# Second-layer weight pieces loaded from GpSimd's queue, and twelve copies of transposed probabilities moved to VectorE

## The chip, the cores and the metric

The kernel runs on one core of a Trainium2 chip. The metric is the device time of one execution in microseconds (us). Before the change, three runs gave a median of 1055.12 us (1054.56 to 1058.52).

## What is computed

Three functions one behind the other, in float32 with float64 weights from the host:

```python
# attention: batch 4, heads 8, sequence 576, head_dim 64
scores = scale * np.matmul(q, k.transpose(0, 1, 3, 2))
scores = np.where(block_i >= block_j, scores, -1000000000.0)   # blocks of 64
attn = np.exp(scores - np.max(scores, axis=-1, keepdims=True))
x = np.matmul(attn / (np.sum(attn, axis=-1, keepdims=True) + 1e-09), v)
x = x.transpose(0, 2, 1, 3).reshape(B * S, H * D)              # 2304 x 512
# first layer, d_ff = 1536
x = ((x @ w_a) * (x @ w_b)) @ w_out
# second layer, d_ff = 1536
xn = x / np.sqrt(np.mean(x * x, axis=-1, keepdims=True) + 1e-06) * rms_g
g = xn @ w_gate
out = (g / (1.0 + np.exp(-g)) * (xn @ w_val)) @ w_out
```

## The kernel before

**Engines and names.** PE multiplies matrices. ACT (ScalarE), DVE (VectorE) and POOL (GpSimd) work on tiles of 128 partitions. SP (SyncE) issues transfers. A float32 operand is split into a high and a low part in a faster format, and a product is three matmuls. Each engine carries out its instructions in the order in which a scheduler placed them when the program was built, and a waiting instruction holds up all behind it on its engine.

**Attention.** Sixteen pairs of heads (four per batch) go through the same steps: PE scores a group of 64 queries of both heads (L455, from batch 2 on L463), DVE takes the row maximum (L478), ACT the exponential into `pp` with its row sum (L484), DVE the reciprocal of the sums (L492, L493), POOL scales `pp` (L496, nine tiles per pair of heads), PE transposes it (L521), and the transposed tile is copied out of PSUM (L523). In batch 0 (`whole`) that copy into `pw` is one ACT copy, and the product with the values follows (L546). In the other batches ACT copies the high part and DVE subtracts to get the low part (L527, values at L590). Batch 0 stands alone in the first 57 us or so. Batches 1 to 3 are interleaved with the matmuls of the first layer (L705 to L707) until about 445 us. The values of a batch are loaded into `vr` (L401) and split on POOL (L114, L427) into `vv`.

**Weights.** Each weight arrives as float64 in a tile of 512 KB, here called a piece. `decode` makes float32 of it: ACT scales the low word in place (L146), ACT turns the high word into `a` (L149), DVE shifts (L150), POOL adds (L151), after which the buffer of the piece is free. The 36 pieces of the second layer use two buffers `st` in turn: 24 of w_gate and w_val ("ab"), each one transfer (L188), and 12 of w_out ("o"), each four transfers of 128 KB (L186). So piece i + 2 can be loaded only when POOL has added piece i. They are decoded in the background of the first layer (4 in its second block, 8 in its third, 24 in its last). Two pieces at a time are combined for a Strassen-Winograd product (`combine`: DVE L233 and L234, POOL L235 and L236, ACT L239 and L240 for the high part, POOL L242 for half of the low part) and stored to DRAM by SP (L244). From about 660 us the second layer streams them back in.

The pieces of the first layer (tiles `ld` and `st`) go through the same function.

Of the kernel before, what the change touches and what calls it, by code (L numbers as in the profile page):

```python
# [12 lines left out]
AF = mybir.ActivationFunctionType  # L13
# [3 lines left out]
P = 128  # L17
# [34 lines left out]
def tile_attention_moe_moe(  # L52
# [13 lines left out]
    pe, act, dve, pool, sp = nc.tensor, nc.scalar, nc.vector, nc.gpsimd, nc.sync  # L66
# [4 lines left out]
    NTH, TF = w_o1.shape[:2]  # L71
# [4 lines left out]
    w_ab, w_o = (w_ab1, w_ab2), (w_o1, w_o2)  # L76
# [48 lines left out]
    gate = {}  # L125
# [46 lines left out]
    def stage_loads(n):  # L172
        while len(staged) + prepared[0] < min(n, len(w_pieces)):
            i = len(staged) + prepared[0]
            layer, kind, f, y = w_pieces[i]
            if layer == 0 and i % LANDING < LANDING - 2:
                if not landing:
                    landing.append(stage.tile([P, LANDING - 2, 4 * P], I64, tag="bg", name="ld", bufs=1))
                st = landing[0][:, i % LANDING]
            else:  # L180
                st = stage.tile([P, 4 * P], I64, tag="st", name="st", bufs=2)
            if kind == "o" and layer == 1:

                for dm in range(KC):
                    z, o = divmod(dm * TF + f % TF, KC)
                    sp.dma_start(out=st[:, dm * P:dm * P + P], in_=w_o[1][f // TF, z, :, o * P:o * P + P])  # L186
            else:
                sp.dma_start(out=st, in_=(w_ab if kind == "ab" else w_o)[layer][f, y])  # L188
            staged[i] = st

    def prepare():

        i = prepared[0]
        if i >= len(w_pieces):
            return
        stage_loads(min(i + min(2 + i, LANDING), max(len(w_pieces) // 2, i + 2)))
        layer, kind, f, y = w_pieces[i]
        w = 4 * P
# [98 lines left out]
    def blocks_of(part, j):  # L297

        return [b for b in PARTS[part] if b >= 2 * j]
# [8 lines left out]
    def attention(pools, x_of, done):  # L308
# [6 lines left out]
        st = [small[:, x, 0:NQ + 2] for x in range(2)]  # L315
# [18 lines left out]
        def single(m):  # L334
            return m >= FIRST_SINGLE
# [163 lines left out]
        def p_transposes(u):  # L499
            m, part = divmod(u, 2)  # L500
            places = PLACE[part]
            whole = m // (H // 2) < WHOLE
            if whole:
                pt[u] = [ap.tile([P, len(places) * P], F32, tag=f"ph{part}", name=f"pw{part}")]
            else:
                pt[u] = [ap.tile([P, len(places) * P], F32R, tag=f"p{x}{part}", name=f"p{x}{part}") for x in "hl"]
            if single(m) and part == 1:

                groups = [[(j, b) for j in js for b in blocks_of(1, j)] for js in ((0,), (1,), (2,), (3, 4))]
            else:  # L510
                groups = [places[at:at + 4] for at in range(0, len(places), 4)]
            at = 0
            for group in groups:
                ps = ps_t()
                n = len(group) * P
                for x, (j, b) in enumerate(group):
                    to = ps[:, x * P:(x + 1) * P]
                    if single(m) and part == 1 and x < 3:
                        by_head = ps[:, 0:3 * P].rearrange("p (h n) -> p h n", h=2)
                        to = by_head[:, :, P:P + Q] if b == NQ - 1 else by_head[:, b % 2, 0:P]  # L520
                    pe.transpose(to, pp[b][:, j * P:(j + 1) * P], ident)  # L521
                hi = pt[u][0][:, at:at + n]
                gate["act"] = act.activation(hi, ps[:, 0:n], AF.Copy)  # L523
                lo = None if whole else pt[u][1][:, at:at + n]
                at += n
                if not whole:
                    dve.tensor_tensor(lo, ps[:, 0:n], hi.bitcast(F32), ALU.subtract)  # L527
                yield n / 1.2
# [76 lines left out]
        ps = ps_s()  # L605
# [7 lines left out]
        for u in range(2 * NP + 2):  # L613
            m, part = divmod(u, 2)
            if u >= 2:
                yield from (whole_values if (u - 2) // H < WHOLE else values)(u - 2)
            sc = list(SCORED[part]) if m < NP else []
            ct = p_transposes(u - 1) if 1 <= u <= 2 * NP else iter(())
            if sc:
                yield score(m, sc.pop(0))  # L620
                if len(sc) > 2:
                    yield score(m, sc.pop(0))
                if part == 0:
                    make_vv(m)
                    make_q(m, 1)
                else:
                    make_k(m + 1)
                    if m + 1 > FIRST_SINGLE:
                        make_q(m + 1, 0)
            alive = True  # L630
            while sc or alive:
                c = next(ct, None) if alive else None
                if c is None:
                    alive = False
                else:
                    yield c
                if sc:
                    yield score(m, sc.pop(0))
            if m < NP and part == 1:
                if m + 1 == FIRST_SINGLE:  # L640
                    make_q(m + 1, 0)
                load(m + 2)
# [348 lines left out]
    n = 0  # L991
# [223 lines left out]
```

## Time and profile before

| | us |
|---|---|
| median of three runs | 1055.12 |
| profiled execution | 1059.24 |
| its span, first to last instruction | 1057.4 |

The profiled execution has 1.84 us around its span and is 4.12 us above the median. PE is busy for 1040.1 us of the span (98%), DVE 697.3 (66%), ACT 618.5 (58%), POOL 426.6 (40%). Busy shares are means over stages with different limits. The rows below are therefore taken stage by stage, and a gap of PE is read by what ended it.

### The profile page before, as it was taken

What the parts mean: (1) busy time and instruction counts of PE and PEld (TensorE: products, weight loads), DVE (VectorE), ACT (ScalarE), POOL (GpSimd) and SP (SyncE); (2) the same over time, 40 slices, a digit from 0 to 9 for tenths busy, and PEclk for the clock granted to TensorE, in tenths of its full rate; (3) what the DMA queues carried; (4) which work ended last, traced back from release to release, by engine and by line L of the source; (5) the groups of instructions that cost most, each with busy time, mean ns of one, the idle gap of its engine ahead of it and who ended that gap; (6) DMA issues with size and microseconds to landing.
All of it is one profiled execution on the core that took longest, in us unless ns stands there. A gap on an engine that the chain in (4) does not pass through costs nothing.

```text
span 1057.4 us, 17005 instructions
## 1 busy us (share of the span) xinstructions
PE 1040.1 (98%) x5676; PEld 934.6 (88%) x5676; DVE 697.3 (66%) x1371; ACT 618.5 (58%) x1376; POOL 426.6 (40%) x448
## 2 busy tenths in 40 slices
PE   9989999999999999999999999999999999999998
PEld 6768887899988888888888888999999999999998
DVE  6547677777775677556587634793876838666285
ACT  7978968577576765456555322753646536355362
POOL 5856667465564564275565501120221202212020
PEclk9999999999999999999999999999999999999999
DMA  9767877978999765798889664787889887887883
GB/s 246 228 185 255 281 257 267 327 258 278 325 342 301 260 234 220 260 344 321 318 314 354 258 224 169 208 287 253 250 289 310 272 269 251 282 277 238 268 249 112
DMA packets 116379, 281.24 MB, mean 266 GB/s; under 512 B 27971, under 2 KB 40771, under 8 KB 105798
## 3 DMA queue, kind: packets, MB, share of 16 engines
q1 hardware_dynamic: 116294, 280.18, 79.6%
q8 instruction: 45, 0.74, 0.3%
q14 instruction: 40, 0.33, 0.1%
HBM read 218.77 MB, written 61.36 MB: 265 GB/s over the span
## 4 chain that ended last, share of the span: by engine, by line
PE 85%; DMA 6%; ACT 4%; DVE 2%; POOL 1%; issue 1%; SPq 0%; ACTq 0%; POOLq 0%
PE mm L733 25%; PE mm L764 12%; PE mm L706 8%; PE mm L707 8%; PE mm L705 8%; PE mm L665 4%; PE mm L667 4%; PE mm L666 4%; PE t L590 3%; PE t L521 3%; PE s L463 2%; DMA qr<-in_q_dram 2%; PE s L455 2%; PE t L546 1%; DMA st<-in_w_o_dram 1%
## 5 line engine op out<-in xcount | busy, mean ns | idle before, releaser
L705 PE MATMUL mm<-xh,ab 128*128 128x512 f32 (+1 forms) x480 | 181.4, 381 | 0.0
L707 PE MATMUL mm<-xh,ab 128*128 128x512 f32 (+1 forms) x480 | 179.7, 374 | 0.0
L706 PE MATMUL mm<-xl,ab 128*128 128x512 f32 (+1 forms) x480 | 179.5, 374 | 0.0
L733 PE MATMUL mm<-hT,w 128*128 128x384 f32 x576 | 165.6, 337 | 1.2 <-ACT mm L741 1.2
L121 POOL TENSOR_TENSOR hl<-g,hh 128x384 fp32r<-128x384 f32 x36 | 42.7, 1187 | 299.7 <-ACT hh L111 299.7
L733 PE MATMUL mm<-hB,w 128*128 128x384 f32 x432 | 125.9, 336 | 0.0
L764 PE MATMUL mm<-hh,w 128*128 128x384 f32 x504 | 125.3, 336 | 0.0
L496 POOL TENSOR_SCALAR pp<-pp,st 128x256 f32<-128x256 f32 (+4 forms) x144 | 84.2, 599 | 73.5 <-DVE st L493 44.1
L741 ACT ACTIVATE mm<-mm 128x384 f32<-128x384 f32 x144 | 66.8, 474 | 75.5 <-PE mm L733 42.5
L733 PEld LDWEIGHTS mm<-hT,w 128*128 128x128 f32 x576 | 105.9, 188 | 2.6 <-ACT mm L741 2.4
L705 PEld LDWEIGHTS mm<-xh,ab 128*128 128x128 f32 x480 | 90.4, 189 | 15.5 <-issue 0.4
L706 PEld LDWEIGHTS mm<-xl,ab 128*128 128x128 f32 x480 | 90.5, 189 | 15.0 <-issue 0.7
L707 PEld LDWEIGHTS mm<-xh,ab 128*128 128x128 f32 x480 | 90.5, 188 | 14.9 <-issue 0.2
L733 PE MATMUL mm<-lT,w 128*128 128x384 f32 x288 | 96.9, 337 | 0.0
L764 PEld LDWEIGHTS mm<-hh,w 128*128 128x128 f32 x504 | 90.7, 188 | 0.3 <-ACT mm L741 0.3
L484 ACT ACTIVATE pp<-s,st 128x288 f32<-128x288 f32 (+8 forms) x142 | 72.3, 512 | 26.3 <-DVE st L478 13.5
L764 PE MATMUL mm<-hl,w 128*128 128x384 f32 x252 | 81.5, 336 | 0.0
L733 PEld LDWEIGHTS mm<-hB,w 128*128 128x128 f32 x432 | 79.5, 188 | 0.0
L665 PE MATMUL mm<-hh,o 128*128 128x512 f32 (+1 forms) x208 | 78.3, 378 | 0.5 <-ACT hh L111 0.5
L666 PE MATMUL mm<-hh,o 128*128 128x512 f32 (+1 forms) x208 | 77.2, 372 | 0.0
L667 PE MATMUL mm<-hl,o 128*128 128x512 f32 (+1 forms) x208 | 75.7, 371 | 0.1
L733 PE MATMUL mm<-lB,w 128*128 128x384 f32 x216 | 72.6, 336 | 0.0
(161 smaller groups left out, 2431.8 us busy)
## 6 DMA issues: line engine op xcount, KB each, us to landing
w<-wc SPq DMA_DIRECT2D x252, 256.0 KB, 3.6
ab<-wab SPq DMA_DIRECT2D x36, 1024.0 KB, 8.7
w<-wco SPq DMA_DIRECT2D x126, 256.0 KB, 3.2
wc<-bg SPq DMA_DIRECT2D x12, 1792.0 KB, 7.3
o<-wo SPq DMA_DIRECT2D x12, 1536.0 KB, 9.5
st<-in_w_ab_dram SPq DMA_DIRECT2D x34, 512.0 KB, 6.8
wab<-ab SPq DMA_DIRECT2D x12, 1024.0 KB, 7.0
wco<-bg SPq DMA_DIRECT2D x6, 1792.0 KB, 6.7
```

The lines of the kernel that those rows point to most:

```text
L121: eng_lo.tensor_tensor(lo, src, hi.bitcast(F32), ALU.subtract)
L484: act.activation(pi[:, a:z], pss[x][:, 0:z - a], AF.Exp, bias=s[:, b:b + 1], scale=1.0, accum_out=t3[:, b, x:x + 1],)
L496: pool.tensor_scalar(t, t, s[:, y:y + 1], 1.0, ALU.mult, ALU.mult)
L665: pe.matmul(ps[:, 0:n], wh, hh, start=(y == 0), stop=False)
L666: pe.matmul(ps[:, 0:n], wl, hh, start=False, stop=False)
L667: pe.matmul(ps[:, 0:n], wh, hl, start=False, stop=(y == TF - 1))
L705: pe.matmul(ps[:, 0:n], wh[:, a:z], xhc, start=(c == 0), stop=False)
L706: pe.matmul(ps[:, 0:n], wh[:, a:z], xlc, start=False, stop=False)
L707: pe.matmul(ps[:, 0:n], wl[:, a:z], xhc, start=False, stop=(c == KC - 1))
L733: pe.matmul(ps, lhs, rhs[:, c, :], start=(start and c == 0 and y == 0), stop=(c == 1 and y == 2), skip_group_check=not start,)
L741: act.activation(to, ps, AF.Copy)
L764: pe.matmul(banks[m], lhs, rhs, start=(start and f == group[0] and y == 0), stop=(f == group[-1] and y == 2), skip_group_check=not start,)
```

## The change

Two edits. In `stage_loads`, the transfers of the second layer's pieces (24 of L188 and 48 of L186) are issued by POOL's queue instead of SP's. Pieces of the first layer stay on SP. In `p_transposes`, for batch 0, a copy whose place in `pw` is not a multiple of eight tiles goes to DVE, without the note for ACT's ordering (`gate`): three of the seven copies of a pair of heads, twelve in all, eight of 128x512 and four of 128x128.

```diff
@@ -183,9 +183,9 @@
                 for dm in range(KC):
                     z, o = divmod(dm * TF + f % TF, KC)
-                    sp.dma_start(out=st[:, dm * P:dm * P + P], in_=w_o[1][f // TF, z, :, o * P:o * P + P])
+                    pool.dma_start(out=st[:, dm * P:dm * P + P], in_=w_o[1][f // TF, z, :, o * P:o * P + P])
             else:
-                sp.dma_start(out=st, in_=(w_ab if kind == "ab" else w_o)[layer][f, y])
+                (pool if layer == 1 else sp).dma_start(out=st, in_=(w_ab if kind == "ab" else w_o)[layer][f, y])
             staged[i] = st
@@ -520,7 +520,10 @@
                 hi = pt[u][0][:, at:at + n]
-                gate["act"] = act.activation(hi, ps[:, 0:n], AF.Copy)
+                if whole and at % (8 * P):
+                    dve.tensor_copy(hi, ps[:, 0:n])
+                else:
+                    gate["act"] = act.activation(hi, ps[:, 0:n], AF.Copy)
```

Lines behind the second edit are three higher after the change (L526 is L523 of before, L598 is L595, L713 is L710). The scheduler places the instructions of all engines anew. At the places that the prediction speaks of, that gives the following.

POOL, around the add of the first second-layer piece (piece 0), between two pairs of heads; `pp_150` to `pp_158` are the nine scaled tiles. Before:

```order
L496 TENSOR_SCALAR pp_156<-pp_156,st 128x512
L496 TENSOR_SCALAR pp_157<-pp_157,st 128x512
L496 TENSOR_SCALAR pp_150<-pp_150,st 128x128
L496 TENSOR_SCALAR pp_151<-pp_151,st 128x128
L496 TENSOR_SCALAR pp_152<-pp_152,st 128x256
L496 TENSOR_SCALAR pp_153<-pp_153,st 128x256
L151 TENSOR_TENSOR src<-src,st 128x512
```

After:

```order
L496 TENSOR_SCALAR pp_156<-pp_156,st 128x512
L496 TENSOR_SCALAR pp_157<-pp_157,st 128x512
L151 TENSOR_TENSOR src<-src,st 128x512
L188 DMA st<-in_w_ab_dram 128x512
L496 TENSOR_SCALAR pp_150<-pp_150,st 128x128
L496 TENSOR_SCALAR pp_151<-pp_151,st 128x128
```

The add and the issue of piece 2's load that it allows now stand ahead of the four small scales instead of behind them.

ACT, the first decode step of the same piece. Before:

```order
L710 ACTIVATE asb<-mm 128x256
L523 ACTIVATE ph_2600<-t 128x384 x3
L484 ACTIVATE pp_152,st<-s,st 128x256
L484 ACTIVATE pp_153,st<-s,st 128x256
L111 ACTIVATE hh<-mm 128x256
L146 ACTIVATE st<-st 128x512
```

After:

```order
L713 ACTIVATE asb<-mm 128x256
L526 ACTIVATE ph_2600<-t 128x384
L146 ACTIVATE st<-st 128x512
L484 ACTIVATE pp_152,st<-s,st 128x256
L526 ACTIVATE ph_2600<-t 128x384
L111 ACTIVATE hh<-mm 128x256
L484 ACTIVATE pp_153,st<-s,st 128x256
```

L146 has moved ahead of two copies, two exponentials and one split. Counted over the whole order in pairs of heads (ten L484 on ACT, nine L496 on POOL), the L149 of piece 2 stood 0.16 of a pair behind the add that frees its buffer and now stands 0.60 behind it; for piece 3 it is 0.60 and 0.62, for piece 4 0.72 and 0.62, for piece 5 0.46 and 0.76.

POOL in the last block of the first layer, at two pieces whose add is followed by loads of two "o" pieces. Before:

```order
L151 TENSOR_TENSOR src<-src,st 128x512 x2
L235 TENSOR_TENSOR src<-src 128x256
L236 TENSOR_TENSOR src<-src 128x256
L242 TENSOR_TENSOR bg<-src,bg 128x3x256
L151 TENSOR_TENSOR src<-src,st 128x2x256
```

After:

```order
L151 TENSOR_TENSOR src<-src,st 128x512
L186 DMA st<-in_w_o_dram 128x128 x4
L151 TENSOR_TENSOR src<-src,st 128x512
L235 TENSOR_TENSOR src<-src 128x256
L186 DMA st<-in_w_o_dram 128x128 x4
L236 TENSOR_TENSOR src<-src 128x256
L242 TENSOR_TENSOR bg<-src,bg 128x3x256
```

Eight issues now stand among the adds and differences of `combine`. In the same stretch, each pair of "ab" loads puts two issues of L188 there. From 445 us on 46 issues (14 of L188, 32 of L186) are POOL's, between 185 and 445 us 26 (10 and 16).

## Rows read from the trace of the kernel before

**Rows 1.** Busy time by stage: start:end, length, busy us of each engine, PEclk, DMA share, GB/s.

```profile
core 0: us, PE busy (x) PEld busy (x) DVE busy (x) ACT busy (x) POOL busy (x), PEclk, DMA share, GB/s
0.00:60.00 60.00, 57.43 (x270) 42.18 (x271) 34.07 (x105) 50.30 (x143) 38.84 (x64) 1.00 0.83 241
...
185.00:235.00 50.00, 49.82 (x308) 44.20 (x307) 36.77 (x88) 32.30 (x88) 24.63 (x37) 1.00 0.87 286
235.00:300.00 65.00, 60.02 (x488) 58.72 (x488) 45.12 (x122) 42.83 (x115) 37.84 (x49) 1.00 0.96 319
300.00:445.00 145.00, 144.53 (x829) 125.77 (x828) 99.23 (x238) 90.50 (x218) 71.54 (x89) 1.00 0.79 266
445.00:600.00 155.00, 155.00 (x682) 127.12 (x681) 105.82 (x151) 81.29 (x132) 92.01 (x69) 1.00 0.87 323
...
660.00:1057.00 397.00, 393.68 (x2253) 391.96 (x2251) 263.74 (x455) 205.95 (x430) 71.82 (x58) 1.00 0.80 254
```

**Rows 2.** What PE waited for, whole span: us in total, times, longest.

```profile
PE s L463 <- ACT pp L484: 5.2, 4, 2.6
...
PE s L455 <- ACT pp L484: 1.2, 3, 0.7
...
PE t L546 <- ACT pw L523: 0.8, 2, 0.5
```

**Rows 3.** Timeline of two stretches, 239:247 and 288:295, ACT and PE.

```profile
242.45 0.66 ACT L149 ACTIVATE a<-st 128x512 f32<-128x512 f32 x1 [3.11 <-DMA st<-in_w_ab_dram]
...
244.13 0.50 PE L463 MATMUL s<-ks,qh 128*128 128x512 f32 x1 [1.71 <-ACT pp L484]
...
289.29 0.40 PE L463 MATMUL s<-ks,qe 128*128 128x288 f32 x1 [0.70 <-ACT pp L484]
...
293.01 0.66 ACT L149 ACTIVATE a<-st 128x512 f32<-128x512 f32 x1 [3.36 <-DMA st<-in_w_o_dram]
...
294.29 0.40 PE L463 MATMUL s<-ks,qe 128*128 128x288 f32 x1 [2.56 <-ACT pp L484]
```

**Rows 4.** Timeline of POOL, 215:262.

```profile
224.64 1.36 POOL L496 TENSOR_SCALAR pp<-pp,st 128x512 f32<-128x512 f32 x2 [3.61 <-DVE st L493]
232.34 1.64 POOL L496 TENSOR_SCALAR pp<-pp,st 128x128 f32<-128x128 f32 x4 [6.34 <-DVE st L493]
233.94 1.31 POOL L151 TENSOR_TENSOR src<-src,st 128x512 uint32<-128x512 uint32 x1
...
250.22 1.37 POOL L496 TENSOR_SCALAR pp<-pp,st 128x512 f32<-128x512 f32 x2 [2.70 <-DVE st L493]
```

**Rows 5.** The chain that ended last, 228:246 and 268:296: start, us, what.

```profile
235.28 7.15 DMA st<-in_w_ab_dram
...
280.25 12.65 DMA st<-in_w_o_dram
```

**Rows 6.** Timeline of SP's queue, 268:296.

```profile
272.50 0.33 SPq L186 DMA_DIRECT2D st<-in_w_o_dram  x1
```

**Rows 7.** Groups by form, whole span: xcount, busy us, mean ns, idle time before.

```profile
L151 POOL TENSOR_TENSOR src<-src,st 128x512 uint32<-128x512 uint32 x36 | 49.6, 1381 | 56.6 <-ACT st L146 37.3 <-DVE src L150 16.7 <-DMA ab<-wab 1.3
...
L235 POOL TENSOR_TENSOR src<-src 128x256 f32<-128x256 f32 x18 | 15.9, 884 | 1.0
```

**Rows 8.** Groups by form, 0:60.

```profile
L523 ACT ACTIVATE pw<-t 128x512 f32<-128x512 f32 x20 | 12.1, 607 | 0.2 <-PE t L521 0.2
...
L478 DVE TENSOR_REDUCE st<-mm 128x1 f32<-128x512 f32 x3 | 2.1, 692 | 1.3 <-PE mm L455 1.2
```

**Rows 9.** Instructions on the buffers `st`: ns min/median/max, first and last start.

```profile
L188 SPq DMA_DIRECT2D st<-in_w_ab_dram x34: 327/333/1217, 17.7 to 572.2; - x34
```

**Rows 10.** Timeline of ACT at the end of the background work, 570:612.

```profile
607.58 0.60 ACT L710 ACTIVATE asb<-mm 128x512 f32<-128x512 f32 x1 [5.13 <-PE mm L707]
```

**Rows 11.** Timeline of POOL and PE, 62:68.

```profile
62.45 0.73 POOL L114 TENSOR_SCALAR vv<-vr 128x640 fp32r<-128x640 f32 x1 [4.80 <-DMA vr<-in_v_dram]
...
66.71 0.33 PE L521 MATMUL t<-ident,pp 128*128 128x128 f32 x1 [2.28 <-POOL pp L496]
```

**Rows 12.** Busy time by stage, right behind that wait (columns as in rows 1).

```profile
67.70:71.10 3.40, 3.40 (x15) 2.93 (x14) 1.20 (x4) 2.33 (x6) 1.54 (x4) 0.50 0.36 140
```

## The prediction

> **What bounds the kernel now.** I read the busy time by stage first [rows 1]. From 660 us to the end PE is busy for 393.68 of 397.00 us, and from 445 to 600 us for all 155.00: there only work of PE itself, or another engine that falls behind, can move the end. The change touches no matmul. What can be won lies where PE has gaps: 57.43 of 60.00 us in the first stage, 60.02 of 65.00 between 235 and 300 us. The list of PE's waits says what ended them: 5.2 us of scores waiting for ACT's exponential, from batch 2 on, and 1.2 + 0.8 = 2.0 us in batch 0 for ACT's exponential and copy [rows 2].
>
> The timeline then shows why ACT was late. At 242.45 its decode step L149 had waited 3.11 us for a piece of second-layer weights, with exponentials queued behind it in order, and PE stood 1.71 us. At 293.01 the same with an "o" piece: 3.36 us on ACT, 2.56 on PE. A third gap of 0.70 us at 289.29 had a load of q ahead of it on ACT, which stays on SP [rows 3]. Those three make 4.97 of the 4.98 us that PE lacks in that stage.
>
> **Part 1a, the loads earlier.** Piece 2's load was issued when POOL had added piece 0: the add ran at 233.94 [rows 4] and the transfer took from 235.28 to 242.43 [rows 5]. So SP's queue cost nothing there; what came late was the add. POOL's order after the change puts it ahead of the four small scales, for which POOL had stood idle 6.34 us from 226.0 on [rows 4], and ACT's L146 moves up likewise. With the two scales that end at 226.0 behind it and L146 two copies and two exponentials earlier, I estimate the add about 5 us sooner, at 229. An issue of 0.9 us (below) and the same 7.15 us of transfer land it near 238.4, and ACT wanted it at 242.45 − 3.11 = 239.3. The margin is 0.9 us: that wait goes, with PE's 1.71 us.
>
> Piece 4 has four transfers. The first was issued at 272.50 [rows 6], the last began at 280.25 [rows 5], 7.75 us later, because other issues lay between them on SP. On POOL they follow each other: 4 × 0.9 = 3.6 us, 4.1 us sooner. But by the order its L149 stands 0.10 of a pair of heads closer to the add, and a pair takes 250.22 − 224.64 = 25.6 us [rows 4], so 2.6 us are given back. Net 1.5 us of the wait of 3.36, and as much of PE's 2.56. The 0.70 us stays. **Term: −1.7 − 1.5 = −3.2 us**; bounds 0 (the loads land as late as before) and −5.0 (all three gaps vanish).
>
> **Part 1b, the price of an issue on POOL.** No row before shows one. From below, SP's own issue: 333 ns median [rows 9]. From above, a POOL operation on a whole piece: 1381 ns mean [rows 7]. I take 0.9 us, near the middle and POOL's own operation on a smaller tile, L235 at 884 ns [rows 7]; both ends are kept.
>
> Between 185 and 445 us POOL has 50 − 24.63 + 65 − 37.84 + 145 − 71.54 = 126 us idle [rows 1], against 26 issues × 0.9 = 23 us. Sixteen of them come as four groups of 3.6 us. A scale queued behind a group would be late only by what exceeds POOL's usual wait for the reciprocal, 2.70 to 3.61 us in the rows at hand [rows 4]: 0.9 us each at most, of which PE sees a part. **Term: +0.5 us**; bounds 0 and 4 × 0.9 = +3.6.
>
> From 445 us on there are 46 issues, 41 us at 0.9 us, beside POOL's 92.01 us of 155 [rows 1]. It fits: 133 of 155. But where two "o" pieces are loaded, 7.2 us of issues stand ahead of L236, on which ACT's combine copy waits in order, ahead of the copies `asb` that PE's buffers need. That happens four times. At the end of the background work ACT had 5.13 us in hand [rows 10]. I put half a microsecond on each place. **Term: +2 us**; bounds 0 and 4 × (7.2 − 5.13 + 1.3) = +13 us, with one add (1.3 us) late on top each time.
>
> **Part 2, the copies.** ACT loses eight of 607 ns [rows 8] and four quarter ones, 4 × 0.15 at least, so about 5.5 us of its 50.30 in the first 60 us; DVE takes them on at 692 ns, the price of its own reading of such a tile from PSUM [rows 8], so about 6.2 us on top of 34.07 [rows 1]. Both have room. Only the 2.0 us of PE's waits in batch 0 [rows 2] can be won, most of them are for the exponential, whose input DVE makes, and DVE now has a copy that can stand ahead of a row maximum. **Term: −0.5 us**; bounds −2.0 and +1.2 (another copy wait of 0.3 us for each of four pairs).
>
> **Sum.** −3.2 + 0.5 + 2 − 0.5 = −1.2 us, on the profiled execution of 1059.24 us as on the median, which lies 4.12 us lower: 1055.1 − 1.2 = **1053.9 us**. One measurement of this kernel tells about 0.5% (5.3 us) from no change, so faster means under 1049.8 and slower over 1060.4.
>
> **A rule weighed against this.** In the rows, SP's issue is short and begins 0.03 us after the add ends at 235.25 [rows 4, 5]. The Trainium skill ("DMA: Bandwidth & Descriptors", section "Issuing engines are not separate DMA queues") says that transfers run on the same 16 engines whichever queue starts them, and that another issuer saves only the time of issuing; by that the sum for 1a would be 0 but for the new order. The trace agrees for piece 2 and does not for piece 4, where the issuing took 7.75 us.
>
> **Rivals.**
> *POOL's issues cost more (slower).* If POOL can be filled to nine tenths of the stretch from 445 us on (a choice: it was 59% full and often waits in turn), the background work ends late once (92.0 + 46 t) / 0.9 exceeds 155 + 5.1 us, that is at t = 1.13 us an issue. At the 1.38 us of an add [rows 7] it is (92.0 + 63.5) / 0.9 = 172.8, 12.7 us late, which takes the place of the +2: 1055.1 − 3.2 + 12.7 = 1064.6; at 1.5 us 1071. For it: the price is not in the trace, and every load waits behind POOL's other work. Against: the stretch has 63 us of POOL idle.
>
> *DVE holds up POOL's issues (slower, within the same case).* The pieces are decoded by DVE while POOL would issue, 619 to 692 ns at a time for such tiles. If each issue waits out one (0.69 us, [rows 8]), t = 0.9 + 0.69 = 1.59 us, (92.0 + 73.1) / 0.9 = 183, 23 us late: about 1075. The Trainium skill ("SBUF — State Buffer", section "SBUF: two separate sides") warns of this: a transfer of GpSimd's queue has its descriptors written by that engine, which a VectorE operation in its two-port mode locks out. No row before has such a transfer, so the trace cannot say.
>
> *The loads are not earlier in effect.* What made the adds late is ACT's and DVE's part of the decoding; if those move with the change, the waits of [rows 3] stay, and POOL's cost is added: 1055.1 + 0.5 + 2 − 0.5 = 1057.1.
>
> *The first stage's big gap closes too.* At 66.71 PE stood 2.28 us for scales that POOL did late because L114 had waited 4.80 us for values [rows 11]; right behind it the granted clock was 0.50 for 3.40 us, the lower of PE's two levels (1.2 of 2.4 GHz), after PE had stood [rows 12], which costs 1.7 us. If the freer ACT or a newly placed load removes that, 4.0 us more go, and with the rest of [rows 3] (5.0 − 3.2 = 1.8) the time is 1048.1. For: everything is placed anew. Against: that load stays on SP.
>
> **Numbers.** Chances: forecast 0.40, its own range 1050 to 1058 (0.08 of it under 1049.8); issues dear, with or without DVE's part, 0.27 (0.25 over 1060.4); loads no earlier 0.15; first gap closed 0.18. So faster 0.26, same 0.49, slower 0.25. The range leaves out the dearest issues and the best of the last case: 1046.5 to 1068.
>
> **What the next profile would show.** Right: POOL rows of L186 and L188 of about 0.9 us; no wait of ACT's L149 for `st` over 1 us near 240 us, about 2 us at the fifth piece; PE near 62 to 63 busy of the 65 us from 235 on and still full from 445 to 600; L523 on DVE at about 0.69 us. Wrong: issues over 1.1 us, or held for longer beside DVE; PE waiting for `asb` or `hh` between 450 and 650 us; the end of layer 1 later than before; scales (L496) late behind groups of four issues.

## The result

The changed kernel took 1062.79 us in the median of six runs (1061.10 to 1065.66), the kernel before 1054.49 us (1052.11 to 1058.52, six runs). The ratio is 1.0072, with a 95% interval of 1.0051 to 1.0092: it is slower, by 8 us. The forecast was 1053.9 us.

The profiled executions were 1063.90 us after and 1059.24 us before. The one of before lies above the median of its kernel, so a second profile of each was taken with the experiments: 1062.17 us (the changed kernel) and 1055.77 us (the kernel before). Where the two pairs differ, the text says so.

The busy time by stage of the changed kernel, in the columns of [rows 1]:

```profile
0.00:75.00 75.00, 70.89 (x334) 53.09 (x335) 48.71 (x139) 57.09 (x161) 50.59 (x78) 1.00 0.82 235
...
235.00:300.00 65.00, 62.31 (x505) 61.16 (x504) 46.91 (x127) 43.54 (x117) 42.45 (x57) 1.00 0.94 328
300.00:360.00 60.00, 52.09 (x292) 45.36 (x291) 37.45 (x92) 35.16 (x87) 32.44 (x41) 0.94 0.69 223
...
445.00:600.00 155.00, 155.00 (x691) 127.45 (x690) 98.08 (x142) 79.59 (x127) 96.27 (x99) 1.00 0.81 301
```

Between 235 and 300 us PE is busy for 62.31 of 65 us where it was 60.02 [rows 1]: in this pair of profiles the gain that the forecast counted on is there in part. From 445 to 600 us PE is full, as before. The loss stands almost wholly in one place, 300 to 360 us: 7.9 us without work for PE, and a granted clock of 0.94, which is 3.6 us lost on 60. In the kernel before the same stretch has neither, in its first profile

```profile
300.00:360.00 60.00, 60.00 (x371) 53.70 (x370) 41.35 (x107) 40.59 (x104) 34.31 (x45) 1.00 0.92 295
```

nor in its second:

```profile
235.00:300.00 65.00, 61.54 (x485) 60.17 (x484) 46.56 (x125) 44.70 (x118) 37.16 (x47) 0.97 0.96 314
300.00:360.00 60.00, 60.00 (x360) 53.23 (x360) 42.64 (x106) 40.88 (x104) 33.28 (x44) 1.00 0.88 288
```

and the second profile of the changed kernel has both again:

```profile
235.00:300.00 65.00, 61.78 (x500) 60.58 (x500) 46.99 (x127) 43.23 (x116) 41.15 (x57) 1.00 0.96 312
300.00:360.00 60.00, 54.38 (x306) 47.82 (x305) 38.65 (x93) 35.94 (x90) 33.88 (x42) 0.94 0.71 231
```

So this stage loses 11.5 us in one profile of the changed kernel and 9.2 us in the other. Of that the kernel wins part back elsewhere: the profiled executions lie 4.7 and 6.4 us apart. In the second pair the gain between 235 and 300 us is almost all in the clock (1.00 for 0.97), for PE is busy there for 61.78 us after and 61.54 before.

The list of PE's waits of the changed kernel (first profile) has these lines, to set beside [rows 2]:

```profile
PE s L463 <- ACT pp L484: 6.0, 3, 4.3
PE mm L668 <- ACT hh L111: 2.1, 3, 1.0
PE mm L670 <- DVE hl L121: 1.9, 1, 1.9
```

Its longest, 4.3 us, is at 343 us. The timeline of all engines there:

```profile
328.26 1.26 SPq L343 DMA_DIRECT2D qr<-in_q_dram  x2
329.62 0.56 SPq L248 DMA_DIRECT2D ab<-wab  x1
330.26 1.25 SPq L361 DMA_DIRECT2D kr<-in_k_dram  x2
...
334.37 0.59 POOL L188 DMA_DIRECT2D st<-in_w_ab_dram  x1 [0.41 <-POOL src L151]
...
335.83 0.33 SPq L248 DMA_DIRECT2D ab<-wab  x1
...
346.53 0.66 ACT L149 ACTIVATE a<-st 128x512 f32<-128x512 f32 x1 [8.19 <-DMA st<-in_w_ab_dram]
...
348.08 0.47 PE L463 MATMUL s<-ks,qh 128*128 128x384 f32 x1 [4.35 <-ACT pp L484]
```

This is the wait of [rows 3] at another piece, piece 6 (the seventh). POOL issued its load 0.41 us after the add, in 0.59 us. It landed 12.1 us later, with two loads of q, two of k and 1 MB of first-layer weights issued by SP ahead of it. ACT stood 8.19 us with its exponentials behind, and PE 4.35 us. In the kernel before, the same decode step had waited 3.86 us in one execution and 0.73 us in the other, and PE had not stood.

The other part of the loss is 40 us earlier, again in the timeline of the changed kernel:

```profile
301.26 1.87 POOL L242 TENSOR_TENSOR bg<-src,bg 128x768 fp32r<-128x768 f32 x1 [2.29 <-ACT bg L239]
...
301.38 2.57 DVE L242 TENSOR_TENSOR bg<-src,bg 128x768 fp32r<-128x768 f32 x1
...
303.09 3.63 POOL L121 TENSOR_TENSOR xl<-xf,xh 128x384 fp32r<-128x384 f32 x3
...
305.55 0.40 DVE L121 TENSOR_TENSOR hl<-mm,hh 128x256 fp32r<-128x256 f32 x1
...
306.00 0.50 PE L670 MATMUL mm<-hl,o 128*128 128x256 f32 x2 [1.93 <-DVE hl L121]
```

DVE's half of the combine's low part, 1.12 us in the mean before and 1.54 us at this place, took 2.57 us beside POOL's half; the low part `hl` that PE wanted was behind it, at the seam of two blocks where the splits of the next block fall due on all engines.

Behind each of the two stalls the granted clock fell, as it had behind the gap at 64 us before [rows 12]. Busy time by stage of the changed kernel, finer:

```profile
308.00:313.00 5.00, 4.64 (x26) 4.13 (x25) 3.95 (x15) 2.45 (x7) 3.64 (x8) 0.72 1.07 431
...
348.00:352.00 4.00, 3.92 (x13) 3.32 (x14) 2.60 (x9) 4.00 (x12) 2.74 (x5) 0.57 0.00 0
```

That is 5 × 0.28 + 4 × 0.43 = 3.1 of the 3.6 us, which PE lost in stretches with part of their time at the lower of its clock's two levels (1.2 of 2.4 GHz), after it had stood; from 304 to 308 us the granted clock was 0.93, 0.3 us more, and the rest is rounding.

The prices that the forecast had to bound, in the groups by form of the changed kernel:

```profile
L186 POOL DMA_DIRECT2D st<-in_w_o_dram x48 | 26.1, 548 | 2.4 <-POOL src L151 1.2 <-issue 1.0
...
L188 POOL DMA_DIRECT2D st<-in_w_ab_dram x24 | 14.0, 583 | 3.1 <-POOL src L151 3.1
...
L524 DVE COPY pw<-t 128x512 f32<-128x512 f32 x8 | 5.5, 689 | 5.9 <-PE t L521 5.7
```

An issue on POOL costs 0.55 to 0.58 us, not 0.9, and a copy on DVE 0.689 us, as forecast.

### The profile page after: what moved, and what is told of

Read it like the earlier page. It is cut to its first block, busy times and chain, and to the rows that moved or that the text cites. A ratio compares the mean times of both kernels' runs of the same rounds, so it can differ in the third digit from the quotient of the medians.

```text
span 1062.0 us, 16982 instructions
## 1 busy us (share of the span) xinstructions
PE 1040.6 (98%) x5676; PEld 936.9 (88%) x5676; DVE 706.1 (66%) x1383; ACT 616.5 (58%) x1364; POOL 462.4 (44%) x520
## 4 chain that ended last, share of the span: by engine, by line
PE 66%; DMA 1%; DVE 0%; ACT 0%; issue 0%; SPq 0%
PE mm L736 25%; PE mm L767 12%; PE mm L710 6%; PE mm L709 6%; PE mm L708 6%; PE mm L669 3%; PE mm L670 3%; PE mm L668 3%; PE t L593 1%; PE s L463 1%; PE t L521 1%; DMA xf<-x_dram 1%; DMA x_dram<-acc 0%; DVE acc L678 0%; PE mm L1025 0%; PE mm L1024 0%
## 5 line engine op out<-in xcount | busy, mean ns | idle before, releaser
L710 PE MATMUL mm<-xh,ab 128*128 128x512 f32 (+1 forms) x480 | 179.5, 375 | 0.0
L496 POOL TENSOR_SCALAR pp<-pp,st 128x256 f32<-128x256 f32 (+4 forms) x144 | 84.6, 600 | 72.7 <-DVE st L493 26.6
L710 PEld LDWEIGHTS mm<-xh,ab 128*128 128x128 f32 x480 | 90.5, 188 | 14.9
L484 ACT ACTIVATE pp<-s,st 128x288 f32<-128x288 f32 (+8 forms) x142 | 72.0, 510 | 30.9 <-DVE st L478 21.9
```

The source lines that it names most:

```text
L484: act.activation(pi[:, a:z], pss[x][:, 0:z - a], AF.Exp, bias=s[:, b:b + 1], scale=1.0, accum_out=t3[:, b, x:x + 1],)
L496: pool.tensor_scalar(t, t, s[:, y:y + 1], 1.0, ALU.mult, ALU.mult)
L710: pe.matmul(ps[:, 0:n], wl[:, a:z], xhc, start=False, stop=(c == KC - 1))
```

## The experiments

Two theories of the loss: **A**, the moved loads cost it where they are (POOL's issues, or landings from its queue). **B**, the new order of all engines costs it, in which ACT or DVE stands in front of something that is not there. **C** put it on the copies. Times are medians; the kernel before was run beside each and its median there is given with the ratio.

**The change in its parts.** Loads alone (both edits of `stage_loads`), copies alone (the edit of `p_transposes`), the single loads alone (line 188), the quarter loads alone (line 186).

> Only the 72 loads move to POOL's queue, the copies stay on ACT. Theory A (the queue itself: a load from POOL is issued later behind POOL's work, about 0.55 us each, and lands later while the transfer engines are full): about 8 us slower than before, near 1062. Theory B (the new order of the whole program, in which ACT's L149 stands ahead of a load that a full set of transfer engines brings late, as the 8.19 us wait at 338 us): between 1050 and 1063, with PE gaps of over 1 us only where ACT's L149 or the like waits for a piece. Theory C (the copies on VectorE cost it): 1054.5, as before.

> Only the twelve copies move to VectorE, all loads stay on SP. Theory A: 1054.5, as before or up to 2 us faster. Theory B: the order is new here too, so the time may move by several us either way though no load changed its queue, and the gaps lie at other places than in batch 0. Theory C: near 1062.

> Only the 24 single loads (L188) move to POOL. Theory A: the loss of the full move in part, 3 to 6 us slower than before, as pieces 2, 3, 6 to 9 are such loads. Theory B: not ordered by how many loads moved; its piece 6 has the same distance to its buffer's add in the order (0.20 of a pair) as in the changed kernel, so a wait of ACT of over 6 us there and a time near 1060.

> Only the 48 quarter loads (L186) move to POOL. Theory A: 3 to 5 us slower than before, since two thirds of the issues move. Theory B: piece 6 is still loaded by SP and stands 0.32 of a pair behind its buffer's add, more than anywhere else, so no long wait there: 1050 to 1056.

| kernel | us | before | ratio | 95% interval |
|---|---|---|---|---|
| loads alone | 1060.51 | 1056.46 | 1.0043 | 1.0022 to 1.0064 |
| copies alone | 1060.15 | 1056.46 | 1.0044 | 1.0027 to 1.0062 |
| 24 single loads | 1063.80 | 1056.46 | 1.0091 | 1.0063 to 1.0119 |
| 48 quarter loads | 1059.13 | 1056.46 | 1.0033 | 1.0017 to 1.0050 |

All four are slower, the copies alone too, with no load moved. 24 moved loads cost at least as much as the 72 that contain them. So the loss isn't a price per moved instruction, and neither A nor C stands alone: A gave 1054.5 for the copies, C 1054.5 for the loads. B's range for these two, 1050 to 1063 for the loads and "several us either way" for the copies, was too wide to fail. Where B was narrower it missed twice: for the single loads it gave a wait of over 6 us at piece 6 (in its profile, its slowest execution at 1071.25 us, ACT waited 2.1 us for piece 6 and at most 4.5 us for any piece that was still on its way, and the median is 1063.8, not 1060), and for the quarter loads 1050 to 1056.

**Holding ACT's decode step behind.** L146 is tied behind ACT's last copies, L149 is not, and so the scheduler puts it early. The edit ties it too; lines behind it are one higher in the kernels that have it.

```diff
         ins = act.activation(lo, lo, AF.Copy, scale=2.0 ** -29)
+        more = act.activation(a, hi.bitcast(F32), AF.Prelu, scale=2.0 ** -111, alpha=-(2.0 ** 32))
         for what in ("act", "hh"):
             behind(ins, what)
-        act.activation(a, hi.bitcast(F32), AF.Prelu, scale=2.0 ** -111, alpha=-(2.0 ** 32))
+            behind(more, what)
```

> The changed kernel, with the first-placed decode step (ACT's L149) kept behind the same copies as L146, so that in ACT's order it stands 0.6 to 2.1 pairs of heads behind the add that frees the buffer (0.20 to 0.76 in the changed kernel). Theory B (ACT stands in order ahead of a load that is not there yet): ACT's waits for pieces between 235 and 445 us fall under 1 us each, the gaps of 1.5 and 4.5 us at 241 and 343 us and the 1.7 us of halved clock behind the second go, about 1055 to 1057. Theory A (loads from POOL cost time where they are): no change, near 1062.

> The kernel before with the same edit. Theory B: the gaps of 1.71 and 2.56 us at 242 and 294 us go, 3 to 5 us faster than before, 1051 to 1053; and the changed kernel with the edit is then within 3 us of this one. Theory A: the edit takes little from either, and the difference between the two stays at 6 to 8 us.

> The kernel before with L149 held behind, and the 72 loads on POOL (copies on ACT). Theory B: within 3 us of the kernel before, 1053 to 1058, though every load is issued by POOL. Theory A: 4 us or more above it.

> The kernel before with L149 held behind, and the twelve copies on VectorE (loads on SP). Theory B: within 3 us of the kernel before, 1053 to 1058, where the copies alone, without the edit, were 3.7 us above it. Theory C (the copies themselves cost it): 4 us above it again.

| with the hold | us | before | ratio | 95% interval |
|---|---|---|---|---|
| changed kernel | 1054.46 | 1056.17 | 0.9981 | 0.9962 to 1.0000 |
| kernel before | 1054.71 | 1056.17 | 1.0001 | 0.9987 to 1.0016 |
| loads alone | 1064.32 | 1054.48 | 1.0070 | 1.0045 to 1.0094 |
| copies alone | 1054.62 | 1054.48 | 1.0000 | 0.9986 to 1.0015 |

In the changed kernel the hold took away the whole loss, and in all four ACT no longer waits for a piece between 235 and 445 us (20.5 us in the changed kernel without it). Busy time by stage of the changed kernel with the hold:

```profile
300.00:360.00 60.00, 57.97 (x328) 50.51 (x327) 42.91 (x100) 37.96 (x94) 35.34 (x44) 0.97 0.74 241
```

5.9 us of PE's gaps in that stage are gone and half of the clock's loss. That much speaks for B, and the copies with the hold, level with the kernel before, speak against C. Two results do not fit B. The kernel before gained nothing from the hold (1.0001), where B gave 3 to 5 us, though PE is busy there for all 65 us between 235 and 300 us: other gaps opened. And the loads alone with the hold are 0.7% above before (9.8 us between the medians; the seven runs lie between 1056.39 and 1068.84). The timeline of that kernel, in the slowest of those runs, shows another load late:

```profile
280.06 1.55 SPq L344 DMA_DIRECT2D qr<-in_q_dram  x2
...
299.77 0.52 ACT L111 ACTIVATE qh<-qr 128x384 fp32r<-128x384 f32 x1 [10.72 <-DMA qr<-in_q_dram]
```

Two loads of q, issued by SP itself behind 2 MB of first-layer weights and beside the pieces from POOL, were awaited for 10.72 us, and PE stood 6.40 us.

**The same kernels again.** Second profiles, told of above.

> The kernel before, unchanged, for a second profile. If the gaps of 1.71 and 2.56 us for pieces at 242 and 294 us belong to the order, they stand here too within half a microsecond; if they hang on how the transfers of an execution happen to fall, one of them is gone or of another size.

> The changed kernel, unchanged, for a second profile. Theory B with a fixed order: the wait of ACT near 338 us for the seventh piece stands at 6 to 9 us again, with a gap of PE of 3 to 5 us. If the landing varies from execution to execution, by over 2 us less or more.

The larger gaps stand at the same places from one execution to the next and change in size by a microsecond or two (before the change, at 242 and 294 us: 1.71 and 2.56 us, then 0.60 and 1.98; after it, at 343 us: 4.35 and 2.40 us, with ACT's wait 8.19 and 6.25 us). The order makes the place; the size goes with the execution. A small one can vanish: behind piece 2 PE stood 1.38 us in the first profile of the changed kernel and not at all in the second.

**Landing by itself.** A kernel of transfers only; the whole computation is left out. The line of the view of the buffer `st` on landing, for the seven settings in turn (microseconds from issue to landing):

> Transfers alone, the whole computation is left out: a piece of 512 KB is loaded six times in each of seven settings, one after the other. (0) from SP alone, (1) from POOL alone, (2) from POOL beside fp32 copies on VectorE, (3) from POOL beside VectorE adds with two inputs, (4) from SP ahead of loads of q, 1 MB, k and another 1 MB, (5) from SP behind the q, 1 MB and k loads and ahead of the last, (6) from POOL, issued when SP has issued the q, 1 MB and k loads. Theory A (POOL's queue is itself slow): (1) lands 2 us or more after (0), and (2) or (3) later still; (6) lands 2 us or more after (5). Theory B with overtaking (what counts is what was issued ahead of the piece): (1) within 1 us of (0), (4) within 2 us of (0), (5) and (6) about alike and some 6 to 8 us later than (4), since 2.2 MB stand ahead at 250 to 330 GB/s.

```profile
DMA to landing us min/median/max: 3.3/3.3/3.5
...
DMA to landing us min/median/max: 3.5/3.6/3.8
...
DMA to landing us min/median/max: 3.9/4.1/4.3
...
DMA to landing us min/median/max: 3.4/3.5/3.5
...
DMA to landing us min/median/max: 3.4/3.6/3.7
...
DMA to landing us min/median/max: 8.3/10.5/11.6
...
DMA to landing us min/median/max: 8.8/9.6/10.1
```

POOL's queue alone adds 0.3 us (3.6 to 3.3); beside fp32 copies on DVE an issue took 0.99 us instead of 0.53 and the landing 0.5 us more; beside adds on DVE nothing. Issued by SP ahead of the q, 1 MB and k loads the piece lands in 3.6 us, behind them in 10.5 us, and from POOL behind them in 9.6 us (there SP had also begun to issue the last 1 MB load, some 0.3 us before POOL's issue). So the queue itself is slower by 0.3 us and no more; what was issued ahead, on whichever queue, decides here. Theory A, as a slow queue, falls.

The Trainium skill ("SBUF — State Buffer", section "A bandwidth-pool intuition that's wrong (but worth ruling out)") puts a transfer from GpSimd's queue at about 620 ns alone and about 3100 ns beside a VectorE copy that locks GpSimd out. The runs agree in the sign and not in the size: 0.46 us more for the issue, with copies of 0.70 us on DVE, and in the changed kernel no issue over 0.73 us.

**Other orders of the same work.** Only the numbers of the interleaving change: attention's share in the second block, or in the first.

```diff
-PACE, AHEAD = (0.49, 1.0, 0.6), (50, 200, 200)
+PACE, AHEAD = (0.49, 1.02, 0.6), (50, 200, 200)
```

> The kernel before with one number of the interleaving changed (attention's share in the second block 1.02 instead of 1.0), which gives the scheduler another order and changes no work and no queue. Theory B (the order decides): it need not stay at the time of the kernel before; it lies anywhere from 1053 to 1062. Theory A (the moved loads decide): within 2 us of the kernel before.

> The same with 0.98. Theory B: 1053 to 1062, and not the same as with 1.02. Theory A: within 2 us of the kernel before.

> The changed kernel with 1.02. Theory B: not tied to the 8 us of the changed kernel, 1053 to 1064; the PE gap behind a waiting piece near 343 us is larger or smaller than 4.5 and 2.6 us. Theory A: 6 us or more above the kernel before with 1.02.

> The changed kernel with attention's share in the first block at 0.50 instead of 0.49; the eighth piece then stands 0.60 of a pair of heads behind its add instead of 0.36. Theory B: 1053 to 1064, and faster than the changed kernel if its piece loads in this order are not stood behind by ACT for over 5 us. Theory A: 1060 to 1064, as the changed kernel.

> The changed kernel with L149 held behind and attention's share in the first block at 0.50, another order of the version that was 1054.5 us. If the hold alone makes the moved loads harmless: 1052 to 1057. If it does not (the loads alone with the hold were 9.8 us above before, by one late load of q): 1058 or more in this order too, with a wait for q of over 5 us.

| kernel | us | before | ratio | 95% interval |
|---|---|---|---|---|
| before, 1.02 | 1054.17 | 1055.13 | 0.9987 | 0.9966 to 1.0007 |
| before, 0.98 | 1057.28 | 1055.13 | 1.0019 | 1.0002 to 1.0036 |
| changed, 1.02 | 1059.94 | 1055.13 | 1.0044 | 1.0026 to 1.0062 |
| changed, 0.50 in the first | 1055.02 | 1055.13 | 1.0002 | 0.9982 to 1.0022 |
| changed, hold, 0.50 in the first | 1063.42 | 1054.69 | 1.0077 | 1.0057 to 1.0097 |

A step of 0.01 in a number that moves no work and no queue takes the changed kernel's whole loss away, and with the hold, which had taken it away too, the same step brings it back. The hold does not make the moved loads harmless. In that last kernel ACT waited 5.2 us for a load of q, as the expectation had it for this outcome; its largest stall of PE is another, at DVE, shown further below.

Neither theory comes out whole. A gave 1060 to 1064 for the changed kernel with 0.50 and missed. But the changed kernel with 1.02 is 5.8 us above the kernel before with 1.02, where A gave 6 or more, and the two other orders of the kernel before lie 1.0 us below and 2.2 us above it, where A gave 2 at most. B made a better time with 0.50 hang on there being no wait of ACT of over 5 us for a piece; the time is better, and there are two such waits, of 5.3 and 6.0 us.

**Whether SP's loads overtake.** In the kernel before, a piece's load stands in SP's queue ahead of the q and k loads and holds them until its buffer is free; off SP's queue it no longer does. The q and k loads of batches 2 and 3 were put on POOL too:

```diff
-                sp.dma_start(out=t[y * D:y * D + D], in_=q[b, 2 * h:2 * h + 2].rearrange("t d s -> d t s"))
+                pool.dma_start(out=t[y * D:y * D + D], in_=q[b, 2 * h:2 * h + 2].rearrange("t d s -> d t s"))
...
-                    sp.dma_start(out=t[rows], in_=k[b, h].rearrange("(t d) s -> d t s", t=2))
+                    pool.dma_start(out=t[rows], in_=k[b, h].rearrange("(t d) s -> d t s", t=2))
```

> The changed kernel, with the loads of q and k of batches 2 and 3 on POOL's queue too, so that SP cannot issue them ahead of a piece whose buffer is not free yet. Theory B with overtaking: the single pieces between 185 and 445 us land 6 to 7.5 us after the add that frees their buffer (8.5 and 9.2 us in the two profiles of the changed kernel, 5.7 and 6.4 us in the kernel before); what the time makes of it depends on the order, 1054 to 1062. Theory A: they land 9 us or more after the add, and the time grows with the 32 further issues on POOL, 1063 or more.

1064.59 us (ratio 1.0088, 1.0066 to 1.0110), and the pieces landed 8.7 us after the add in the mean, one of them 20 us after. A's time came (1063 or more), and neither theory's landing did (9 us or more, 6 to 7.5). That overtaking is the cause of the later landing isn't borne out by the mean. For piece 6 alone the runs agree with it: it landed 6.9 us after the add here, 12.5 and 10.6 us in the changed kernel.

**A faster one.** The edits without a loss of their own: copies on DVE, the hold, 1.02, and all loads on SP.

> Copies on VectorE, all loads on SP, L149 held behind, attention's share in the second block at 1.02: the three edits without a loss put together. If they add up, 1050 to 1053, faster than the kernel before; if each is only an order like others, 1053 to 1058.

1052.20 us beside 1054.69, ratio 0.9970 (0.9958 to 0.9982): it beats both kernels, by 2.5 and by some 10 us. In its stages:

```profile
235.00:300.00 65.00, 62.49 (x504) 61.10 (x502) 51.81 (x131) 47.55 (x127) 43.35 (x53) 1.00 0.99 342
300.00:360.00 60.00, 58.84 (x333) 51.10 (x334) 36.13 (x98) 35.54 (x88) 29.83 (x39) 1.00 0.73 247
```

The gain before 300 us is there (2.5 us against the first profile of the kernel before, 1.0 us against the second), the loss behind it is 1.2 us, and the clock stays up. That the three edits add up isn't shown: 1.02 alone gave 0.9987 (0.9966 to 1.0007), and that interval overlaps with this one.

## Why the prediction was wrong

**The steps that failed** are two: the transfer time in part 1a, and, larger, a term that the sum does not have.

In part 1a it is "an issue of 0.9 us and the same 7.15 us of transfer land it near 238.4". The order did what was read from it: POOL's add of piece 0 stood at 228.49, where 229 was estimated, and the issue ran from 230.09 to 230.69. But from issue to landing it took not 7.15 us but 11.1, and the wait stayed. Timeline of the changed kernel, with SP's two loads of 1 MB ahead:

```profile
224.10 4.64 SPq L248 DMA_DIRECT2D ab<-wab  x2
...
230.09 0.60 POOL L188 DMA_DIRECT2D st<-in_w_ab_dram  x1 [0.30 <-POOL src L151]
...
241.25 0.66 ACT L149 ACTIVATE a<-st 128x512 f32<-128x512 f32 x1 [4.25 <-DMA st<-in_w_ab_dram]
```

It landed at 241.2 where before, issued 5.2 us later, it landed at 242.4 [rows 5]. ACT, for its part, wanted it at 241.25 − 4.25 = 237.0 and not at 239.3. The second profile has the same with other sizes: 8.5 us from issue to landing, where the second profile of the kernel before has 6.0, and ACT waited 1.69 us.

```profile
230.03 0.60 POOL L188 DMA_DIRECT2D st<-in_w_ab_dram  x1 [0.30 <-POOL src L151]
...
238.61 0.69 ACT L149 ACTIVATE a<-st 128x512 f32<-128x512 f32 x1 [1.69 <-DMA st<-in_w_ab_dram]
```

The transfer engines were 0.96 busy in that stage [rows 1]. In the kernel before, the issue of the two loads of 1 MB had ended 4.3 us before that of the piece began:

```profile
226.30 4.66 SPq L248 DMA_DIRECT2D ab<-wab  x2
```

In the changed kernel it had ended 1.4 us before. More of the 2 MB was then still ahead of the piece, and it waited there instead. The time from issue to landing was not the load's own but, for the most part, the backlog's.

For the time of the whole, this counts for little: PE's gap behind piece 2 went from 1.71 to 1.38 us in one pair of profiles and from 0.60 us to nothing in the other. The larger step is what the sum leaves out. Only the waits that PE had felt in one execution were taken through the new order. Piece 6, which ACT awaited before without a gap of PE, was not looked at, and it made the 4.35 us and 1.7 us of slow clock. The seam at 301 to 309 us, with its gaps of 0.99 and 1.93 us for PE and the slow clock behind them, wasn't looked at either. Put in general: the sum priced the removal of three known gaps, the issues and the copies, and gave the order of everything else a price of nothing, without a reason; the runs showed 11.5 and 9.2 us in the one stage from 300 to 360 us.

**The rule that was weighed against it** said that another issuer saves only issuing time, by which part 1a "would be 0 but for the new order". For piece 2 that is what came. For piece 4 the earlier issues did count, and by more than the 1.5 us of the forecast. All four were issued within 2.21 us, the last landed 10.9 us after the add that frees the buffer (20.4 us before), and in both profiles after the change the wait (3.36 and 2.78 us before) is gone:

```profile
271.37 2.21 POOL L186 DMA_DIRECT2D st<-in_w_o_dram  x4
...
282.23 0.69 ACT L149 ACTIVATE a<-st 128x512 f32<-128x512 f32 x1
```

**The other terms.** The price of an issue: 0.55 to 0.58 us measured, 0.9 taken. The tail: +2 us forecast, none came, PE is full from 445 to 600 us with 46 issues on POOL. The rival of dear issues, the only one beyond 1060.4, had the wrong place and the wrong price; its sign was right by chance. No issue waited out a DVE operation of 0.69 us, as its second form had it: the longest took 0.73 us. That the measured 1062.79 lies inside the range of 1046.5 to 1068 is owed to that rival too. The copies: 0.689 us each as forecast (0.692). In their stage PE is busy for 70.89 and 69.76 of 75 us in the two profiles after, 69.94 and 70.21 before, so a term of −0.5 us can be neither seen nor ruled out. Their own order costs 4 us alone and nothing with the hold. Busy time by stage, the kernel before (first and second profile) and the second profile of the changed kernel:

```profile
0.00:75.00 75.00, 69.94 (x322) 51.56 (x323) 39.55 (x120) 59.72 (x169) 48.66 (x77) 0.98 0.76 216
0.00:75.00 75.00, 70.21 (x336) 51.87 (x336) 40.94 (x125) 61.31 (x173) 49.17 (x77) 1.00 0.79 225
0.00:75.00 75.00, 69.76 (x331) 51.55 (x332) 48.84 (x138) 56.96 (x160) 50.09 (x77) 1.00 0.81 231
```

The lower clock behind the gap at 64 us, on which the rival of the first stage rested, is absent after the change, but also in the second profile before it: so nothing shows that the change took it away.

**What is shown and what stays open.** Ten kernels have loads on POOL: they are 0.50% above the kernel before in the mean of their ratios (0.9981 to 1.0091). Six others keep them on SP: 0.04% (0.9970 to 1.0044). So, as an estimate from these sixteen, a move of such loads costs about 5 us in the mean of the orders tried, and the order that comes with it some 4 us to either side; the 8 us would be both. The orders were not drawn at random, and not all ten move the same loads. Four pairs differ in the 72 loads alone: without other edits, with the copies, with the hold, and with both, the loads on POOL are 0.43, 0.28 and 0.69% above and 0.19% below the same kernel with them on SP, in the mean 0.30%, or 3 us. A price of the move is therefore likely, but four pairs, one of them the other way, do not settle it. For the mean there are two signs in the traces, both worked out from all their rows. First, the single loads between 185 and 445 us land 8.0 us after the add that frees their buffer in the ten profiles of kernels with them on POOL (7.1 to 9.2), and 6.0 us (5.4 to 7.1) in nine with these loads on SP; about half of the 2.0 us is that the issue begins later (1.0 us after the add against 0.06), since POOL's other work stands in front of it. The other half isn't settled: the queue alone gives 0.3 us, and the trial with q and k on POOL did not bring it back. A later landing does not cost by itself: in the changed kernel with the hold it is 7.9 us, and nothing is lost.

Second, DVE is held longer. In the eight profiles with all loads on SP, the longest to which an operation of DVE with two operands in SBUF was drawn out between 185 and 445 us is 2.57 us. In six of eleven with loads on POOL it is 4.4 to 5.8 us (not in the changed kernel itself, where it is 2.57 us again; and the changed kernel with the hold, which loses nothing, is one of the six, with 4.57). The timelines of three of the six, first with the quarter loads alone on POOL:

```profile
295.03 5.33 DVE L242 TENSOR_TENSOR bg<-src,bg 128x768 fp32r<-128x768 f32 x1
```

then with q and k on POOL as well:

```profile
301.08 5.81 DVE L121 TENSOR_TENSOR xl<-xf,xh 128x384 fp32r<-128x384 f32 x1
301.85 3.75 POOL L121 TENSOR_TENSOR xl<-xf,xh 128x384 fp32r<-128x384 f32 x5
305.57 0.86 POOL L121 TENSOR_TENSOR ql<-qr,qh 128x128 fp32r<-128x128 f32 x2
306.39 1.89 POOL L427 TENSOR_TENSOR vv<-vr,vv 128x640 fp32r<-128x640 f32 x1
```

and the changed kernel with hold and 0.50:

```profile
302.27 5.11 DVE L412 SCALAR_TENSOR_TENSOR ks<-kr,ks 64x1152 fp32r<-64x1152 f32 x1 [0.18 <-ACT ks L410]
```

PE waited 5.9 us for DVE's additions behind the second, and 5.5 us in two waits behind the third. In both, a group of four issues had ended on POOL less than four us earlier. That POOL's issues push its other work together and so make these holds longer is argued from where they stand; no run shows it by itself.

## What to carry to other kernels

Where the transfer engines are as full as here (0.96), a load need not land sooner by as much as it is issued sooner: piece 2 gained 1.2 us from 5.2 in one pair of profiles, while piece 4 gained its whole wait. Read what is in flight ahead of a load, not how long it took before. Where a scheduler places everything anew, look for the waits that an in-order engine had in hand without a gap, and try two or three neighbours of a number of the interleaving for both kernels before a difference under one per cent is put down to the edit. Ask of a wait of 4 us not only what it costs but what it does to the clock behind it.

## What the runs showed of the hardware

An operation of DVE with both operands in SBUF can stand while POOL carries out several such operations one behind another: 0.54 us became 5.81 us beside seven splits of POOL in a row, and it was done while POOL's next one (L427) was drawn out in its turn, 1.89 us where it took 1.56 us elsewhere. The Trainium skill ("SBUF — State Buffer", section "Who interferes with whom") states this for a VectorE instruction with two SBUF inputs against a GpSimd instruction that reads SBUF; the traces here agree, and show that a hold can outlast several of POOL's instructions.

One execution's profile can lie 4 us above its kernel's median, with gaps at the same places and of other sizes: the kernel before gave 1059.24 and 1055.77 us in its two.
